# w_out loaded a second time, one byte further, in a fused convolution and SoLU kernel

## The chip, the cores and the metric

The kernel runs on 1 core of a Trainium2 chip. The time is the device time of one execution in microseconds (us). The kernel before takes 1151.21 us, the median of 3 runs (1150.63 to 1151.89).

Five engines work side by side, each through its own list of instructions in order: TensorE (PE; PEld is its weight load), VectorE (DVE), ScalarE (ACT), GpSimd (POOL) and SyncE (SP), which issues DMAs here.

## What is computed

```
w   = softmax(weight, over the 7 taps)                 # 8 heads x 7
x   = causal 7-tap convolution of x by w, head by head # 33280 tokens x 192
h   = x @ w_in                                         # 192 x 1024
sm  = exp(h - max h) / (sum + 1e-9)
s   = h * sm
ln  = (s - mean s) / sqrt(var s + 1e-6) * g_ln         # over 1024
out = (ln @ w_out) in float32                          # 1024 x 192
```

x, weight and g_ln are float32. w_in and w_out are float64; the kernel sees them as pairs of 32-bit words (low, high) and converts them itself.

## The kernel before, in words

The tokens are cut into 260 tiles of 128 (NT). For each tile TensorE multiplies the convolved rows by w_in in halves of float16 (`emit_rows` L747, `emit_first` L758, `emit_third` L779; the result `ph` is 128x1024 in PSUM); VectorE scales it and takes the maximum (`emit_max` L812, row L815), ACT the exponential (`emit_exp` L819, L822), VectorE the numerator (`emit_mul` L830, L832), ACT or POOL its upper half and POOL its lower half in float16 (`emit_hi` L837, `emit_lo` L857), SyncE turns both by a DMA transpose (`pT`, L860), TensorE multiplies by `ohl`, the halves of w_out (`emit_out` L877, L890), and VectorE empties the result. The accumulators in PSUM are three pairs of banks, so the product of tile 3 takes the pair of tile 0 and waits for that tile's numerator.

Every instruction's place in its engine's list is written out by hand (the schedule is manual): the program's order is each engine's order. `first_two`, `second_two`, `third_two` and `fourth_two` emit tiles 0 to 7 two by two, mixed with what is left of the start; then `three_steps` runs over three tiles at a time, and `last_three` ends it.

The start loads x for chunk 0, w_in (`raw_in`), and w_out (`raw_out`, L402), all from SyncE; then, later, x for chunks 1 and 2 with g (`gl`, L653) between them. A double becomes a float32 in class `Words`. For w_out, `wo`, in this order: `exponents` (VectorE, L467: the exponent bits of the high word), `powers` (ACT, L507: the power of two they stand for), `lows` (POOL, L478: the low word as a float), `mantissas` (VectorE, L472: 20 bits of the high word and the leading one), `floats` (ACT, L484: that integer as a float), `whole` (POOL, L495: plus the low word), `signs` (VectorE, L510: the sign bit into the power), `out_powers` (ACT, L702: eight products of the power by g, one for each block of 128 rows), `squares` (ACT, L490: the sum of squares, from which the scale `t_out` follows), `value` (POOL, L517: float times power, in two halves). From `out_scale` on, TensorE takes the mean over the rows of w_out (L718), VectorE subtracts it (L727), ACT and VectorE make the two halves `ohl` (L732, L736).

The order that the change touches is in `first_two`: `emit_first`, the maximum and exponential of tile 0, then `mantissas`, `floats`, `whole` and `signs` of w_out, the numerator of tile 0, `out_powers`, the maximum and exponential of tile 1, `squares`, the upper half of tile 0, `settle_rest` (VectorE's lower halves of the second part of chunk 0, L329, and their transposes into `yT`), the numerator of tile 1.

Buffers turn by tag. Tag `xs` has two: `raw_in`, then `f_in`; then `f_out` takes that of `raw_in`. Tag `g_raw` has three, for the exponents and mantissas of w_in and w_out and later for results.

Of the kernel before, what the change touches and what calls it, by code (L numbers as in the profile page):

```python
# [9 lines left out]
F32 = mybir.dt.float32  # L10
BF16 = mybir.dt.bfloat16
I32 = mybir.dt.int32
U32 = mybir.dt.uint32
AF = mybir.ActivationFunctionType
# [6 lines left out]
def kernel(  # L21
# [10 lines left out]
    P = 128  # L32
# [345 lines left out]

    w_in, w_out = w_in.bitcast(I32), w_out.bitcast(I32)
# [28 lines left out]
    rebias = cp.tile([P, 1], F32, name="rebias")  # L408
    pool.memset(rebias, -916.0 * 2.0**23)
    act.activation(rebias[0:1], rebias[0:1], AF.Copy)  # L410
    mhalf = cp.tile([P, 1], F32, name="mhalf")
# [35 lines left out]
    class Words:  # L447


        def __init__(self, raw, name):  # L450
# [4 lines left out]
            self.f = xp.tile(  # L455
                [P, NWM * D], F32, name=f"f_{name}", tag="xs", bufs=2
            )[:, 0:n]

        def exponents(self, c):
            if self.e is None:  # L460
                self.e, self.m = (
                    sp.tile(
                        [P, GMAX * D], I32, name=f"{q}_{self.name}", tag="g_raw", bufs=3
                    )[:, 0 : self.n]
                    for q in "em"
                )
            dve.tensor_scalar(  # L467
                self.e[:, c], self.high[:, c], 0x7FF00000, None, ALU.bitwise_and
            )
# [7 lines left out]
        def lows(self, c, scale):  # L477
            pool.tensor_scalar(  # L478
                self.low[:, c].bitcast(F32), self.low[:, c], scale, 1.0,
                ALU.mult, ALU.mult,  # L480
            )

        def floats(self, c):
            act.copy(self.m[:, c].bitcast(F32), self.m[:, c])  # L484

        def squares(self, c, to):
# [3 lines left out]
            act.activation(  # L490
                junk, self.e[:, c].bitcast(F32), AF.Square, scale=2.0**20, accum_out=to
            )

        def whole(self, c):
            pool.tensor_tensor(  # L495
                self.f[:, c], self.m[:, c].bitcast(F32),
                self.low[:, c].bitcast(F32), ALU.add,
            )
# [7 lines left out]
        def powers(self, c):  # L506
            act.activation(self.e[:, c], self.e[:, c], AF.Relu, bias=rebias, scale=8.0)  # L507
# [11 lines left out]
    wi, A, Z = Words(raw_in, "in"), slice(0, F), slice(F, 3 * F // 2)  # L519
# [8 lines left out]
    def valued(c, eng=pool):  # L528

        wi.signs(c, wi.m)  # L530
        wi.value(c, wi.m, eng)
# [108 lines left out]
    wo, W = Words(raw_out, "out"), slice(0, NFC * D)  # L640
# [8 lines left out]
    valued(Z)  # L649
    settle(*spans0[0], got1)  # L650
# [32 lines left out]
    wo.lows(W, 2.0**-32)  # L683
# [8 lines left out]
    osq = cp.tile([P, 1], F32, name="osq")  # L692
# [4 lines left out]
    def out_powers():  # L697


        woe = wo.e.bitcast(F32).rearrange("p (c d) -> p c d", d=D)  # L700
        for j in range(NFC):
            act.activation(  # L702
                woe[:, j], woe[:, j], AF.Copy, scale=gl[:, j : j + 1]
            )
# [476 lines left out]
    def first_two():  # L1181
# [5 lines left out]
        wo.mantissas(W)  # L1187
        wo.floats(W)
        wo.whole(W)
        wo.signs(W, wo.e)  # L1190
        emit_mul(t)
        out_powers()
        emit_max(u)
        emit_exp(u)
        wo.squares(W, osq)
        emit_hi(t)
        settle_rest()
        emit_mul(u)
# [470 lines left out]
```

## Time and profile before

| | us |
|---|---|
| median of 3 runs | 1151.21 |
| the profiled execution, its own time | 1150.31 |
| its span (first to last instruction) | 1148.6 |
| TensorE busy | 1127.5 |
| VectorE busy | 994.3 |
| ScalarE busy | 989.2 |
| GpSimd busy | 891.9 |

The profile is one execution recorded by the hardware profiler. A busy time is the sum of an engine's instructions without its waits. A timeline lists instructions by start, adjacent ones of a kind merged with their count; in brackets is how long the engine stood idle before and what ended that. The granted clock is 1.00 of full speed in every stretch shown.

### The profile page before, as it was taken

Reading aid. Unit: us, or ns where it says so; the run is one execution under the profiler, and the core shown is the slowest. Engines: PE = TensorE matmul, PEld = TensorE weight load, DVE = VectorE, ACT = ScalarE, POOL = GpSimd, SP = SyncE. Lnnn points to the kernel's source line nnn. Section 1 sums busy time; section 2 is a strip of 40 time slices with the busy share of each in tenths; the row PEclk is TensorE's granted clock in tenths of the full one; section 3 lists DMA queues with packets and bytes.
Section 4 is the critical chain, followed back from the end, with each engine's and each line's share of the span. In section 5 each row is a group of like instructions: output and inputs, shape, how many; then the busy total and the mean of one; then the engine's idle time right before and its main releaser. Section 6 shows DMA issues by size and latency. Waiting matters only on the chain.

```text
span 1148.6 us, 22366 instructions
## 1 busy us (share of the span) xinstructions
PE 1127.5 (98%) x7729; PEld 688.3 (60%) x7729; DVE 994.3 (87%) x2024; ACT 989.2 (86%) x1789; POOL 891.9 (78%) x711
## 2 busy tenths in 40 slices
PE   5999999999999999999999999999999999999998
PEld 3675556665666566656666666565656666566556
DVE  8889898988888898888888988888888887888787
ACT  7888998888888888988889898888888889888885
POOL 3866899978788687888868788687888868855664
PEclk9999999999999999999999999999999999999999
DMA  7999999999999999999999999999999998989977
GB/s 228 189 187 184 200 210 205 215 209 210 199 210 205 192 211 200 218 188 210 199 197 197 211 201 204 195 211 202 193 211 194 205 196 164 182 161 189 190 154 179
DMA packets 727424, 226.95 MB, mean 198 GB/s; under 512 B 651647, under 2 KB 725903, under 8 KB 727311
## 3 DMA queue, kind: packets, MB, share of 16 engines
q1 hardware_dynamic: 727310, 225.53, 102.7%
q8 instruction: 60, 0.98, 0.3%
q14 instruction: 54, 0.43, 0.1%
HBM read 33.00 MB, written 25.56 MB: 51 GB/s over the span
## 4 chain that ended last, share of the span: by engine, by line
PE 89%; ACT 2%; DVE 2%; DMA 2%; POOL 2%; issue 1%; SPq 0%; DVEq 0%; ACTq 0%; POOLq 0%
PE po L890 41%; PE ph L753 37%; PE pc L288 6%; PE ph L782 5%; DMA pT<-p 1%; POOL p L858 1%; ACT sq L847 1%; DMA raw_in<-in_moe_w_in_dram 1%; POOL xs L250 1%; DVE ph L815 0%; ACT e L822 0%; DVE e L832 0%; POOL xr L247 0%; ACT p L843 0%; ACT e_out L702 0%
## 5 line engine op out<-in xcount | busy, mean ns | idle before, releaser
L858 POOL TENSOR_TENSOR p<-e,p 128x1024 f16<-128x1024 f32 x257 | 547.7, 2135 | 188.3 <-ACT p L843 187.4
L890 PE MATMUL po<-ohl,pT 128*128 128x192 f16 (+1 forms) x4264 | 539.5, 283 | 3.1 <-DVE raw L900 1.4
L890 PEld LDWEIGHTS <-pT 128*128 128x128 f16 x4264 | 384.2, 98 | 163.2 <-issue 4.1
L753 PE MATMUL ph<-whi,yT 128*128 128x512 f16 x1548 | 419.0, 380 | 1.5 <-DVE e L832 1.5
L815 DVE TENSOR_SCALAR_CACHE_REDUCE ph<-ph,cv 128x1024 f32<-128x1024 f32 x248 | 319.3, 1289 | 87.0 <-PE ph L782 68.8
L822 ACT ACTIVATE e<-ph,sm 128x1024 f32<-128x1024 f32 x260 | 289.1, 1112 | 99.8 <-DVE ph L815 92.2
L832 DVE SCALAR_TENSOR_TENSOR e<-ph,cv,e 128x1024 f32<-128x1024 f32 x248 | 317.1, 1279 | 24.4 <-ACT e L822 23.9
L753 PEld LDWEIGHTS <-yT 128*128 128x128 f16 x2064 | 192.9, 98 | 228.5 <-issue 35.3
L843 ACT CAST p<-e 128x1024 f16<-128x1024 f32 x245 | 254.3, 1038 | 25.9 <-DVE e L832 23.0
L847 ACT ACTIVATE sq<-e 128x1024 f32<-128x1024 f32 x260 | 273.2, 1051 | 0.2
L753 PE MATMUL ph<-wlo,yT 128*128 128x512 f16 x516 | 153.5, 379 | 0.0
L900 DVE TENSOR_REDUCE raw<-po 128x192 f32<-128x384 f32 x247 | 136.9, 554 | 15.6 <-PE po L890 15.3
L250 POOL TENSOR_TENSOR xs<-xr,xs 128x960 f16<-128x960 f32 (+1 forms) x56 | 107.5, 1919 | 1.3
L782 PE MATMUL ph<-wlo,yT 64*128 64x512 f16 x269 | 74.1, 380 | 0.0
L329 DVE SCALAR_TENSOR_TENSOR y<-pc,y 112x432 f16<-112x432 f32 (+5 forms) x140 | 72.2, 533 | 0.9 <-ACT y L320 0.7
L288 PE MATMUL pc<-xs,taps_hi 128*112 128x240 f16 (+1 forms) x448 | 72.9, 261 | 0.0
L320 ACT ACTIVATE y<-pc 112x432 f16<-112x432 f32 (+5 forms) x140 | 62.6, 468 | 10.0 <-PE pc L288 5.5
L782 PE MATMUL ph<-wlo,y 64*128 64x512 f16 x251 | 68.7, 380 | 0.0
L183 DVE TENSOR_REDUCE xa<-xr 128x1 f32<-128x384 f32 x112 | 66.7, 618 | 0.0
L288 PEld LDWEIGHTS <-taps_hi 128*112 128x112 f16 x448 | 52.3, 130 | 16.0
L247 POOL TENSOR_SCALAR xr<-xr,s 128x960 f32<-128x960 f32 (+1 forms) x56 | 57.4, 1025 | 3.3 <-ACT xs L241 0.4
L288 PE MATMUL pc<-xs,taps_lo 128*112 128x240 f16 (+1 forms) x224 | 58.5, 261 | 0.0
(155 smaller groups left out, 774.4 us busy)
## 6 DMA issues: line engine op xcount, KB each, us to landing
out_dram<-raw SPq DMA_DIRECT2D x127, 192.0 KB, 3.0
xr<-in_x_dram SPq DMA_DIRECT2D x41, 480.0 KB, 4.9
xr<-in_x_dram SPq DMA_DIRECT2D x22, 384.0 KB, 4.3
pT<-p SPq DMA_TRANSPOSE x263, 4.6
y<-yT SPq DMA_DIRECT2D x15, 140.0 KB, 2.8
y<-yT SPq DMA_DIRECT2D x15, 126.0 KB, 2.9
yT<-y SPq DMA_TRANSPOSE x102, 3.7
raw_out<-in_moe_w_out_dram SPq DMA_DIRECT2D x1, 1536.0 KB, 10.3
```

Of the source, the lines that this page charges most:

```text
L250: (2.1 * size + 0.2, lambda: pool.tensor_tensor(xl, r, h, ALU.subtract)),
L288: nc.tensor.matmul(o, tp[:, h + j, :], r, start=q == 0, stop=q == len(ops) - 1)
L753: nc.tensor.matmul(bank, lhs, w[:, r, n * 512 : (n + 1) * 512], start=start and j == 0, stop=stop and j == len(ops) - 1,)
L782: nc.tensor.matmul(banks_of(t)[n], y[q, t.off : t.off + P], wlo[q, 1, n * 512 : (n + 1) * 512], start=start, stop=not start,)
L815: dve.tensor_scalar(t.ph, t.ph, t.cv[:, 0:1], None, ALU.mult, ALU.min, accum_out=t.bias)
L822: act.activation(t.e, t.ph, AF.Exp, bias=t.bias, scale=-1.0, accum_out=grp.z[:, g : g + 1])
L832: dve.scalar_tensor_tensor(t.e, t.ph, t.cv[:, 3:4], t.e, ALU.mult, ALU.mult, accum_out=t.grp.s1[:, t.g : t.g + 1],)
L843: act.copy(t.p16[:, :, 0, :], t.halves)
L847: act.activation(junk, t.e, AF.Square, accum_out=t.grp.s2[:, t.g : t.g + 1])
L858: eng.tensor_tensor(t.p16[:, :, 1, :], t.halves, t.p16[:, :, 0, :], ALU.subtract)
L890: nc.tensor.matmul(t.po[:, 0:n], t.pT[:, a, :], w, start=j == 0, stop=j == len(ops) - 1)
L900: dve.tensor_reduce(t.grp.raw[:, t.g, :], t.po[:, 0 : 2 * D].rearrange("p (a d) -> p d a", a=2), AX.X, ALU.add,)
```

## The change

w_out is loaded a second time, now from ACT's queue, into a tile `raw_top` of which the DMA fills the bytes from 1 on. The second word of each pair of words there (`shifted`) holds bytes 3 to 6 of the double, that is the lower 24 bits of its high word and the upper 8 of its low word: 28 bits of the mantissa in one word. `tops` on VectorE masks them and sets the leading one; `floats` turns this integer to a float on ACT, in eight pieces with g as the scale. So `lows`, `whole`, `mantissas` (for w_out) and `out_powers` go, and the float is written over the integers. `rebias_out` moves the exponent by 8 for the larger integers. The sum of squares is now taken of the powers without g, scaled by the largest g times 2^28 (`out_largest`: one reduction of `gl` on VectorE, one scaling on POOL). In `first_two` the numerator of tile 0 and the maximum of tile 1 come ahead of `signs`, and the numerator of tile 1 ahead of `settle_rest`. The load is issued behind the two `whi` rows of w_in on ACT; its buffer is that of `raw_in` (tag `xs`).

```diff
+    out_bytes = w_out.bitcast(U8)
...
+    fixed = cp.tile([P, 3], F32, name="fixed")
+    rebias, rebias_out, mhalf = (fixed[:, j : j + 1] for j in range(3))
...
+    pool.memset(rebias_out, -924.0 * 2.0**23)
...
-        def lows(self, c, scale):
...
-        def floats(self, c):
-            act.copy(self.m[:, c].bitcast(F32), self.m[:, c])
...
+        def tops(self, c):
+            dve.tensor_scalar(
+                self.m[:, c], self.shifted[:, c], 0xFFFFFFF, 0x10000000,
+                ALU.bitwise_and, ALU.bitwise_or,
+            )
+
+        def floats(self, c, by):
+            act.activation(self.f[:, c], self.m[:, c], AF.Copy, scale=by)
...
-        def whole(self, c):
...
-    wo, W = Words(raw_out, "out"), slice(0, NFC * D)
+    raw_top = xp.tile([P, NWM * D], I32, name="raw_top", tag="xs", bufs=2)
+    shifted = raw_top[:, 0 : 2 * NFC * D].rearrange("p (f t) -> p f t", t=2)[..., 1]
+    wo, W = Words(raw_out, "out", rebias_out, shifted), slice(0, NFC * D)
...
     for c in halves:
         act.activation(whi[:, 0, c], wi.f[:, c], AF.Copy, scale=t_in)
     valued(Z)
+    act.dma_start(
+        raw_top.bitcast(U8)[:, 1 : 1 + 8 * NFC * D].rearrange("p (c b) -> p c b", c=NFC),
+        out_bytes.rearrange("(c p) b -> p c b", p=P),
+    )
...
-    wo.lows(W, 2.0**-32)
...
-    def out_powers():
...
+    def out_floats():
+
         for j in range(NFC):
-            act.activation(
-                woe[:, j], woe[:, j], AF.Copy, scale=gl[:, j : j + 1]
-            )
+            wo.floats(slice(j * D, (j + 1) * D), gl[:, j : j + 1])
+
+    def out_squares():
+
+        wo.squares(W, osq, gm)
+
+    def out_largest():
+
+        dve.tensor_reduce(gm, gl, AX.X, ALU.max, apply_absolute_value=True)
+        pool.tensor_scalar(gm, gm, 2.0**28, 1.0, ALU.mult, ALU.mult)
...
         emit_exp(t)
-        wo.mantissas(W)
-        wo.floats(W)
-        wo.whole(W)
+        wo.tops(W)
+        out_largest()
+        out_floats()
+        emit_mul(t)
+        emit_max(u)
         wo.signs(W, wo.e)
-        emit_mul(t)
-        out_powers()
-        emit_max(u)
         emit_exp(u)
-        wo.squares(W, osq)
+        out_squares()
+        emit_mul(u)
         emit_hi(t)
         settle_rest()
-        emit_mul(u)
         emit_hi(u)
```

## Rows read from the trace of the kernel before

**Rows 1.** The page: the first line, and the line of busy time, share of the span and instructions of each engine.

```profile
span 1148.6 us, 22366 instructions
PE 1127.5 (98%) x7729; PEld 688.3 (60%) x7729; DVE 994.3 (87%) x2024; ACT 989.2 (86%) x1789; POOL 891.9 (78%) x711
```

**Rows 2.** The view of waits for TensorE over the whole span: engine and line that waited, engine and line waited for; us in total, times, longest us.

```profile
PE ph L753 <- DVE e L832: 1.5, 1, 1.5
PE pc L288 <- issue: 1.7, 1, 1.7
PE po L890 <- DVE raw L900: 1.4, 2, 0.9
PE po L890 <- DMA pT<-p: 1.1, 3, 0.4
```

**Rows 3.** The timeline of TensorE between 27 and 45 us: start us, duration us, engine, line, operation, out<-in, shape, count, and in brackets the idle time before with what ended it. The second row is the first output product (tile 0), the third that of tile 1.

```profile
27.93 0.61 PE L753 MATMUL ph<-whi,yT 128*128 128x512 f16 x2 [1.48 <-DVE e L832]
...
41.66 2.15 PE L890 MATMUL po<-ohl,pT 128*128 128x192 f16 x24 [0.24 <-ACT xj L189]
...
44.36 2.15 PE L890 MATMUL po<-ohl,pT 128*128 128x192 f16 x24 [0.40 <-DMA pT<-p]
```

**Rows 4.** The chain of waits in the first 60 us: start us, us, what.

```profile
26.70 2.88 ACT e_out L702 x8
...
39.52 0.45 DVE ohl L736
```

**Rows 5.** The timeline of VectorE from 22 to 42 us, columns as in rows 3. L815 is the maximum of a tile (tiles 1 and 2), L832 its numerator (tiles 0 and 1), L329 the lower halves of chunk 0, L727 and L736 the centring of w_out and its low half.

```profile
23.83 1.18 DVE L472 TENSOR_SCALAR m_out<-raw_out 128x1536 int32<-128x1536 int32 x1
24.93 1.74 DVE L510 SCALAR_TENSOR_TENSOR e_out<-raw_out,e_out 128x1536 int32<-128x1536 int32 x1
26.59 1.27 DVE L832 SCALAR_TENSOR_TENSOR e<-ph,cv,e 128x1024 f32<-128x1024 f32 x1
...
27.79 1.28 DVE L815 TENSOR_SCALAR_CACHE_REDUCE ph<-ph,cv 128x1024 f32<-128x1024 f32 x1
...
29.00 1.46 DVE L329 SCALAR_TENSOR_TENSOR y<-pr,s,y 112x480 f16<-112x480 f32 x3
30.70 1.28 DVE L832 SCALAR_TENSOR_TENSOR e<-ph,cv,e 128x1024 f32<-128x1024 f32 x1 [0.25 <-ACT e L822]
...
31.91 1.29 DVE L815 TENSOR_SCALAR_CACHE_REDUCE ph<-ph,cv 128x1024 f32<-128x1024 f32 x1
...
37.57 1.81 DVE L727 SCALAR_TENSOR_TENSOR f_out<-f_out,mean 128x768 f32<-128x768 f32 x2
39.52 1.95 DVE L736 SCALAR_TENSOR_TENSOR ohl<-f_out,t_out,ohl 128x768 f16<-128x768 f32 x2
```

**Rows 6.** The timeline of GpSimd (POOL) from 20 to 45 us and, last, TensorE's mean of w_out; columns as in rows 3.

```profile
22.57 1.62 POOL L478 TENSOR_SCALAR raw_out<-raw_out 128x1536 f32<-128x1536 uint32 x1
26.70 3.54 POOL L495 TENSOR_TENSOR f_out<-m_out,raw_out 128x1536 f32<-128x1536 f32 x1 [2.52 <-issue]
...
30.41 3.58 POOL L517 TENSOR_TENSOR f_out<-f_out,e_out 128x768 f32<-128x768 f32 x2
...
33.95 2.85 PE L718 MATMUL mean<-f_out,even 128*128 128x192 f32 x16
```

**Rows 7.** The timeline of ScalarE (ACT) from 14 to 36 us, and POOL's row that it waits for; columns as in rows 3.

```profile
15.83 1.33 ACT L648 ACTIVATE whi<-f_in,t_in 128x512 f16<-128x512 f32 x2 [0.45 <-DVE t_in L114]
16.73 1.26 POOL L517 TENSOR_TENSOR f_in<-f_in,m_in 128x512 f32<-128x512 f32 x1 [0.63 <-DVE m_in L510]
18.03 2.94 ACT L660 ACTIVATE whi<-f_in,t_in 64x512 f16<-64x512 f32 x4 [0.87 <-POOL f_in L517]
...
25.11 1.46 ACT L484 CAST m_out<-m_out 128x1536 f32<-128x1536 int32 x1
```

**Rows 8.** DMA. First from the page: the queues that carried data, and the issue of raw_out (KB, us from issue to landing). Then SyncE's timeline (start us, us of the issue). Then busy times by stretches: the stretch, its length, the busy time of each engine, the granted TensorE clock, the share of the 16 DMA engines' time in which they were busy, GB/s. Last the packets of the stretch from 24.75 to 25.75 us.

```profile
q1 hardware_dynamic: 727310, 225.53, 102.7%
...
raw_out<-in_moe_w_out_dram SPq DMA_DIRECT2D x1, 1536.0 KB, 10.3
...
5.72 0.42 SPq L402 DMA_DIRECT2D raw_out<-in_moe_w_out_dram  x1
...
20.16 1.14 SPq L162 DMA_DIRECT2D xr<-in_x_dram  x2
21.35 0.52 SPq L653 DMA_DIRECT2D gl<-in_moe_g_ln_dram  x1
...
12.00:15.00 3.00, 2.38 (x15) 2.08 (x15) 2.67 (x10) 2.65 (x8) 0.54 (x1) 1.00 1.05 366
15.25:15.50 0.25, 0.25 (x5) 0.25 (x4) 0.20 (x2) 0.13 (x1) 0.25 (x1) 1.00 0.09 31
17.20:18.50 1.30, 0.84 (x4) 0.33 (x5) 1.30 (x4) 0.47 (x1) 0.79 (x1) 1.00 0.00 0
18.50:22.50 4.00, 2.97 (x11) 0.62 (x9) 3.50 (x7) 3.91 (x8) 0.41 (x3) 1.00 0.53 98
21.25:21.50 0.25, 0.06 (x1) 0.07 (x2) 0.25 (x1) 0.25 (x1) 0.00 (x0) 1.00 0.27 40
22.50:25.75 3.25, 3.25 (x15) 1.12 (x14) 3.13 (x4) 3.07 (x4) 1.69 (x2) 1.00 1.15 303
...
DMA packets 1303, 0.19 MB, mean 194 GB/s; under 512 B 1056, under 2 KB 1303, under 8 KB 1303
```

More of the change, by code (lines that the diff above doesn't have):

```diff
@@ L13 @@
 U32 = mybir.dt.uint32
+U8 = mybir.dt.uint8
 AF = mybir.ActivationFunctionType
@@ L405 @@
     )
-    rebias = cp.tile([P, 1], F32, name="rebias")
+    fixed = cp.tile([P, 3], F32, name="fixed")
+    rebias, rebias_out, mhalf = (fixed[:, j : j + 1] for j in range(3))
     pool.memset(rebias, -916.0 * 2.0**23)
     act.activation(rebias[0:1], rebias[0:1], AF.Copy)
-    mhalf = cp.tile([P, 1], F32, name="mhalf")
+    pool.memset(rebias_out, -924.0 * 2.0**23)
     pool.memset(mhalf, -0.5)
@@ L447, with __init__ @@
     class Words:
-        def __init__(self, raw, name):
+        def __init__(self, raw, name, bias, shifted=None):
+            self.bias, self.shifted = bias, shifted
             self.name = name
@@ L454, in __init__ @@
             self.n, self.e = n, None
-            self.f = xp.tile(
-                [P, NWM * D], F32, name=f"f_{name}", tag="xs", bufs=2
-            )[:, 0:n]
+            if shifted is None:
+                self.f = xp.tile(
+                    [P, NWM * D], F32, name=f"f_{name}", tag="xs", bufs=2
+                )[:, 0:n]
         def exponents(self, c):
@@ L466, in exponents @@
                 )
+                if self.shifted is not None:
+                    self.f = self.m.bitcast(F32)
             dve.tensor_scalar(
@@ L475, in mantissas, with squares @@
             )
-        def lows(self, c, scale):
-            pool.tensor_scalar(
-                self.low[:, c].bitcast(F32), self.low[:, c], scale, 1.0,
-                ALU.mult, ALU.mult,
-            )
-        def floats(self, c):
-            act.copy(self.m[:, c].bitcast(F32), self.m[:, c])
-        def squares(self, c, to):
+        def tops(self, c):
+            dve.tensor_scalar(
+                self.m[:, c], self.shifted[:, c], 0xFFFFFFF, 0x10000000,
+                ALU.bitwise_and, ALU.bitwise_or,
+            )
+        def floats(self, c, by):
+            act.activation(self.f[:, c], self.m[:, c], AF.Copy, scale=by)
+        def squares(self, c, to, scale=2.0**20):
             junk = sp.tile([P, F], F32, name=f"oj_{self.name}_{c.start}", tag="sq", bufs=1)
@@ L490, in squares @@
             act.activation(
-                junk, self.e[:, c].bitcast(F32), AF.Square, scale=2.0**20, accum_out=to
-            )
-        def whole(self, c):
-            pool.tensor_tensor(
-                self.f[:, c], self.m[:, c].bitcast(F32),
-                self.low[:, c].bitcast(F32), ALU.add,
+                junk, self.e[:, c].bitcast(F32), AF.Square, scale=scale, accum_out=to
             )
@@ L506, in powers @@
         def powers(self, c):
-            act.activation(self.e[:, c], self.e[:, c], AF.Relu, bias=rebias, scale=8.0)
+            act.activation(self.e[:, c], self.e[:, c], AF.Relu, bias=self.bias, scale=8.0)
         def signs(self, c, to):
@@ L517, in value @@
             eng.tensor_tensor(f, f, powers[:, c].bitcast(F32), ALU.mult)
-    wi, A, Z = Words(raw_in, "in"), slice(0, F), slice(F, 3 * F // 2)
+    wi, A, Z = Words(raw_in, "in", rebias), slice(0, F), slice(F, 3 * F // 2)
     HF = F // 2
@@ L682 @@
     wo.powers(W)
-    wo.lows(W, 2.0**-32)
+    both = cp.tile([P, 2], F32, name="gm_osq")
+    gm, osq = both[:, 0:1], both[:, 1:2]
     def settle_rest():
@@ L691 @@
     t_out = cp.tile([P, 1], F32, name="t_out")
-    osq = cp.tile([P, 1], F32, name="osq")
     wof = wo.f.rearrange("p (c d) -> p c d", d=D)
@@ L695 @@
     out_halves = [slice(0, NFC * D // 2), slice(NFC * D // 2, NFC * D)]
-    def out_powers():
-        woe = wo.e.bitcast(F32).rearrange("p (c d) -> p c d", d=D)
+    def out_floats():
         for j in range(NFC):
-            act.activation(
-                woe[:, j], woe[:, j], AF.Copy, scale=gl[:, j : j + 1]
-            )
+            wo.floats(slice(j * D, (j + 1) * D), gl[:, j : j + 1])
[4 more added lines that the diff above has]
+        pool.tensor_scalar(gm, gm, 2.0**28, 1.0, ALU.mult, ALU.mult)
     def out_scale():
```

## The prediction

> **What bounds the kernel now.** I read the page's busy times first. TensorE is busy 1127.5 of 1148.6 us [rows 1]: the kernel can hardly gain in its body, and what it can gain or lose lies in TensorE's pauses. The view of what TensorE waited for puts nearly all of them before 45 us; of its waits on the output products only 1.4 and about 0.7 us come later (its three waits for `pT` total 1.1, of which one of 0.4 is at 44.36) [rows 2, 3]. Since the body is TensorE-bound, a microsecond by which the first output products move is a microsecond of the whole.
>
> So the change must be judged in the start, where tiles 0 to 3 share the engines with the conversion of `w_out`. TensorE's row list shows it there waiting for others: 1.48 us for tile 0's numerator (L832), 0.24 and 0.40 us ahead of the first two output products [rows 3]. Who is late? The chain of waits runs over ACT's multiplication by g at 26.70 and DVE's low half of `ohl` at 39.52 [rows 4]. VectorE's own rows settle it: from 23.83 to the end of that low half at 41.47 they stand end to end, with one listed pause of 0.25 us inside [rows 5]. VectorE's queue carries the start; ACT and POOL matter only when a VectorE row has to wait for them.
>
> **What goes.** On POOL the low words (1.62 us) and the sum of halves (3.54 us) vanish [rows 6], on ACT the cast of 1.46 us, since the eight multiplications by g (2.88 us for all, 0.36 each) now read the integers themselves [rows 4, 7]. I value all of this at nothing. POOL has no row that holds VectorE up here: its value of `f_out` (3.58 us from 30.41) feeds the mean at 33.95, but the mean is only used at 37.57, when VectorE has finished both numerators [rows 5, 6]. After the change the value waits for `signs`, and 3.58 us of POOL and 2.85 us of mean need some 6.5 us between the end of `signs` and L727. VectorE's own work there covers it: 6.87 us from tile 1's numerator at 30.70 to L727 at 37.57, and the 1.46 us of lower halves that now stand there too. Without that cover the mean would be the next to be late.
>
> **What stays on VectorE.** The top words cost what the mantissas cost (L472, a step of 1.10 us from 23.83 to 24.93): same form, same stride. The maximum of g, a 128x8 reduction, has no row; its nearest are the small reductions and scalars of the same view at 0.15 to 0.21 us, I take 0.2. `signs` (a step of 1.66 us, 24.93 to 26.59) only moves behind the maximum of tile 1. If everything had landed, tile 0's numerator could then start once tile 0's exponential is through (25.1, when ACT's next row starts), not at 26.59; but the list from there to the maximum of tile 2 then holds `signs` again. Before: numerator at 26.59, maximum of tile 2 at 31.91, so 5.32 us, of which 0.25 is a pause. After: 5.32 - 0.25 + 1.66 = 6.73 us [rows 5, 7]. From tile 2's maximum on VectorE's list is the same as before. With data in hand the start ends within 0.1 us of where it does now, and only the 0.40 us at the second output product is there to win: at best about -0.4 us. Work is taken from the engines that wait, none from the one that is waited for.
>
> **What is added: two landings in VectorE's way.** The extra memset and the 128x1 scaling of the maximum on POOL lie in idle time there. The second load is 1536 KB. Its buffer is the one of `raw_in`, free after VectorE's last `signs` of w_in, which ends at about 16.65 (the value of that piece starts on POOL at 16.73). ACT issues it behind the two `whi` rows, which end at 17.16; ACT then stands until 18.03 in any case [rows 7]. SyncE's issues of such loads take about 0.5 us [rows 8]; ACT's are not in this trace (one dynamic queue is used), so between 0 and 0.87 us it costs nothing, and I take it as free.
>
> When does it land? SyncE's load issued at 20.16 shows its first packets at about 21.35, 1.2 us later; the same delay here gives 18.4. The load of `raw_out` moved at 366 GB/s with all 16 DMA engines busy, so 1.573 MB are 4.30 us of them. From 17.2 to 18.5 they are free, from 18.5 to 22.5 busy for 0.53 of the time with `yT` transposes and the first x rows: 0.1 + 0.47 x 4.0 = 2.0 us. After 22.5 they are full (1.15). So 2.3 us of the load are left over when the x rows of chunk 1, and behind them g, want the same engines [rows 8].
>
> And g is now waited for on VectorE. Its load is issued on SyncE at 21.35 behind two x loads; its 1024 packets of 4 bytes are the 1056 small ones of 24.75 to 25.75. In the kernel before only ACT at 26.70 needs it, and it does not wait. After, the reduction of g stands between the top words and tile 0's numerator. Whichever of the two streams the engines prefer, both are through only after 25.75 + 2.3 = 28.05; with about 0.5 us to landing (`raw_out`'s packets end at 15.5, it landed at 5.72 + 10.3 = 16.0) that is 28.55 [rows 8]. If g is last, 0.2 us follow, if the top words are last, 1.3 us: the numerator starts at 28.8 to 29.9, I take the middle, 29.3.
>
> By the Trainium skill, "DMA: Bandwidth & Descriptors", section "Issuing engines are not separate DMA queues", a load issued by another engine runs on the same 16 DMA engines and interleaves with the rest, so that only issue time is saved; no run here shows two queues. By it the sum stands as it is; without it the load would cost what the first rival below does.
>
> Behind the waiting top words are queued on VectorE tile 0's numerator, tile 1's maximum, `signs`, tile 1's numerator and the lower halves of chunk 0; TensorE (tile 3 needs tile 0's numerator), ACT and POOL wait for those. **The sum**: (29.3 - 26.59) + (1.66 - 0.25) = 4.1 us at the maximum of tile 2, and as much at the first output product, 41.66; less the 0.40 us at the second product, whose transpose is then no longer last: +3.7 us. The bounds of the same sum are 28.8 and 29.9: +3.2 and +4.3. The transposes of `yT` that tile 0 needs may come up to 1 us later by the sharing, which the wait of the top words covers. The profiled run took 1150.31 us (its span and 1.7 us around it), 0.9 us under the median; on the median of 1151.21 the forecast is 1154.9.
>
> **Rivals.** *The load fits into the gaps*: not slower. If it never holds up g, g still lands at 25.75 + 0.4, the reduction ends at 26.35, and the sum is 26.35 - 26.59 + 1.41 - 0.4 = +0.8 us, 1152.0. The place is the reduction of g on VectorE; it decides as long as the numerator of tile 0 starts before 27.9, where the sum reaches 2.3 us, 0.2%, about what a measurement of this kernel tells from no change. For it: the engines are free about half of the time until 22.5, and in what order they serve two streams is in no row. Against it: nothing before 17.16 can start it, and whichever stream goes first, the other is the later by it.
>
> *The odd address halves the rate.* All loads of this trace start on whole words, so none prices it. At twice 4.30 us (an assumed factor, the mildest that would matter much), 6.6 us would be left at 22.5, the top words would start at 25.75 + 6.6 + 0.5 = 32.85, the numerator at 34.2, and the sum is 7.6 + 1.41 - 0.4 = +8.6 us: 1159.8. The Trainium skill, "DMA: Bandwidth & Descriptors", section "How a descriptor splits into AXI transactions", says that a descriptor starting off a 256-byte boundary needs a further transaction; it says so of reads, and no row here shows it for a write. Seven for six would by estimate add 0.7 us, 1155.6.
>
> *The delay is paid back.* TensorE waits for 2.1 us on others after 45 us; if those releasers are not delayed as much, since POOL and ACT have 6.6 us less to do, at most these come back: +1.6 us, 1152.8. Against it: the delayed engine is the one that feeds all of them.
>
> *Faster.* TensorE's pauses between 27 and 45 us are 2.1 us and the 1.7 us ahead of the convolution L288 [rows 2, 3], and VectorE's list sets when they end; 2.3 us would need VectorE itself to run quicker. The mantissas took 1.18 us beside POOL, and the passes that leave POOL cover 5.2 us; even a fifth less of that is 1.0 us, which with the first rival gives -0.2 us.
>
> **How the numbers follow.** The forecast 0.50; the load in the gaps 0.26; half rate 0.13; paid back 0.07; faster by more than 0.2% by something that I don't see 0.04. Slower is 0.50 + 0.13 = 0.63, same 0.26 + 0.07 = 0.33, faster 0.04. The range goes from just under the first rival's 1152.0 to the half-rate case: 1151.6 to 1160.0.
>
> **What would show it.** Right: in the profile after, VectorE has a pause of 3 to 5 us ahead of the top words or of the reduction of g, ended by a DMA; tile 0's numerator starts near 29.3; the first output product near 45.8; ACT's load is issued near 17.2 without delaying the row at 18.03; POOL stands idle longer, without effect. Wrong: the top words start before 26, or the load takes over 12 us to land, or TensorE's pauses after 45 us shrink by what the start lost.

## The result, and the profile after

The changed kernel took 1157.2 us (median of 6 runs, 1156.56 to 1159.03), the kernel before 1151.55 us in the 6 runs beside them (1150.63 to 1153.8): ratio 1.0051, 95% interval 1.0041 to 1.0061, so 5.65 us slower. Forecast was 1154.9 us within 1151.6 to 1160.0, with slower as the likeliest. Sign and range held; the size was 2 us short, and the profile shows that the wait on which the sum stood is not the one that was paid. That the number came so near is in good part luck.

The profiled run of the changed kernel took 1159.03 us around a span of 1157.3. The two spans differ by 8.7 us, since this run lies 1.8 us over the median of its kernel and the profiled run of before (1150.31 us) 1.2 us under its own. Times inside the trace are therefore read as to where the loss sits, the timed runs as to how much it is.

First TensorE, since the body hangs on it: its waits over the whole span (engine and line that waited, engine and line waited for; us in total, times, longest us), and its timeline (start us, us, engine, line, operation, out<-in, shape, count, idle before).

```profile
PE ph L777 <- DMA yT<-y: 5.5, 2, 4.1
PE po L902 <- DMA pT<-p: 3.2, 1, 3.2
...
PE po L902 <- DVE raw L912: 1.4, 2, 0.9
PE ph L765 <- DVE e L844: 1.0, 1, 1.0
```

```profile
24.14 1.89 PE L777 MATMUL ph<-whi,yT 128*128 128x512 f16 x4 [4.14 <-DMA yT<-y]
...
48.84 4.02 PE L902 MATMUL po<-ohl,pT 128*128 128x192 f16 x24 [3.18 <-DMA pT<-p]
...
52.99 2.97 PE L902 MATMUL po<-ohl,pT 128*128 128x192 f16 x24
```

Two waits are new or many times longer: 4.1 us for a transpose of y (`yT`, the input of tile 0's logits), and 3.2 us for the transpose of tile 0's weights (`pT`). Both are transfers that the change does not touch. The first output product starts at 48.84 where it started at 41.66, the second at 52.99 where it started at 44.36 [rows 3]: +7.2 and +8.6 us, and with the second the difference of the spans is complete. The waits for `raw` are the same 1.4 us as before [rows 2]: what follows 55 us was not changed.

Next VectorE, whose list the prediction followed. L827 is a tile's maximum, L485 the top words, L715 the new reduction of g, L844 a tile's numerator, L511 the signs, L330 the lower halves of chunk 0.

```profile
14.67 0.15 DVE L647 TENSOR_REDUCE isq<-pt_wi 128x1 f32<-128x3 f32 x1
...
27.02 1.29 DVE L827 TENSOR_SCALAR_CACHE_REDUCE ph<-ph,cv 128x1024 f32<-128x1024 f32 x1 [5.15 <-PE ph L794]
...
28.23 0.96 DVE L485 TENSOR_SCALAR m_out<-raw_top 128x1536 int32<-128x1536 int32 x1
29.10 0.15 DVE L715 TENSOR_REDUCE gm_osq<-gl 128x1 f32<-128x8 f32 x1
29.72 1.28 DVE L844 SCALAR_TENSOR_TENSOR e<-ph,cv,e 128x1024 f32<-128x1024 f32 x1 [0.46 <-ACT e L834]
...
32.13 1.75 DVE L511 SCALAR_TENSOR_TENSOR e_out<-raw_out,e_out 128x1536 int32<-128x1536 int32 x1
33.81 1.27 DVE L844 SCALAR_TENSOR_TENSOR e<-ph,cv,e 128x1024 f32<-128x1024 f32 x1
...
35.01 1.46 DVE L330 SCALAR_TENSOR_TENSOR y<-pr,s,y 112x480 f16<-112x480 f32 x3
36.39 1.28 DVE L827 TENSOR_SCALAR_CACHE_REDUCE ph<-ph,cv 128x1024 f32<-128x1024 f32 x1
```

The pause of 5.15 us stands one step earlier than forecast: ahead of tile 0's maximum, not ahead of the top words, and it ends with TensorE's logits. Top words and reduction of g follow without any wait: both loads had landed. The same rows of the kernel before, to set beside them (the first is the reduction of a norm of w_in that stands ahead of all that the change touches, the second the maximum of tile 0):

```profile
14.89 0.15 DVE L644 TENSOR_REDUCE isq<-pt_wi 128x1 f32<-128x3 f32 x1
...
22.62 1.29 DVE L815 TENSOR_SCALAR_CACHE_REDUCE ph<-ph,cv 128x1024 f32<-128x1024 f32 x1 [0.52 <-PE ph L782]
```

The starts of the executions differ: that reduction stands at 14.67 to 16.53 us in the profiles of this study. Where stages of several kernels are compared below, I count from it. Tile 0's maximum is at 22.62 - 14.89 = 7.73 us before, and at 27.02 - 14.67 = 12.35 after: 4.6 us later. In the trace's own times, tile 0's numerator stands at 29.72 (forecast 29.3), tile 2's maximum at 36.39 instead of 31.91 [rows 5]: +4.5 (forecast +4.1). The numbers fit, by another cause: the pause is not VectorE's wait for a landing.

That cause is on the DMA side. First the load's issue on ACT with ACT's next `whi` row (timeline of ACT), then the issues (KB, us from issue to landing), then packets, MB and share of the 16 engines of each queue between 19 and 22 us: after (first two lines), and the same stretch before (last fence). q10 is the queue of the new load, q1 that of SyncE, where all other data goes.

```profile
16.46 0.42 ACTq L653 DMA_DIRECT2D raw_top<-in_moe_w_out_dram  x1
17.81 2.94 ACT L667 ACTIVATE whi<-f_in,t_in 64x512 f16<-64x512 f32 x4 [0.87 <-DVE y L330]
```

```profile
raw_top<-in_moe_w_out_dram ACTq DMA_DIRECT2D x1, 1536.0 KB, 7.2
...
gl<-in_moe_g_ln_dram SPq DMA_DIRECT2D x1, 4.0 KB, 6.0
```

```profile
q10 hardware_dynamic: 723, 1.11, 102.7%
q1 hardware_dynamic: 28, 0.01, 1.1%
```

```profile
q1 hardware_dynamic: 1108, 0.30, 55.5%
```

The issue cost ACT nothing (`whi` follows at 17.81, before at 18.03 [rows 7]). The load landed at 16.46 + 7.2 = 23.7 us, 4.6 us before VectorE came to it. But while it ran, SyncE's queue had 28 packets in 3 us, all of them after 21.5 us, where it had 1108 before. The chain of waits (start us, us, what) shows what stood there:

```profile
17.38 6.71 DMA yT<-y
41.24 7.55 DMA pT<-p
```

The transpose of y issued at 17.38 took 6.71 us; before, the one issued at 18.90 landed in 2.49, and the one ahead of it in 2.5. In the kernel before, TensorE went on with tile 0's logits at

```profile
21.44 0.61 PE L765 MATMUL ph<-whi,yT 128*128 128x512 f16 x2 [0.69 <-DMA yT<-y]
```

after it did so at 24.14, 2.7 us later, and from there to the maximum it took 2.9 us instead of 1.2, with four instead of two of the large matmuls left and, as the next view shows, at half the clock: 4.4 us in all in the trace's own times, 4.6 counted from the reduction. The busy times of three stretches (stretch, length, busy time of each engine, granted clock, DMA share, GB/s) show both the full engines and what TensorE ran at behind its waits:

```profile
18.50:22.50 4.00, 1.18 (x4) 0.29 (x3) 3.28 (x6) 3.91 (x8) 0.53 (x3) 1.00 1.02 345
24.00:27.00 3.00, 2.86 (x7) 0.60 (x8) 0.00 (x0) 0.00 (x0) 0.00 (x0) 0.50 1.14 319
48.00:52.90 4.90, 4.06 (x26) 3.86 (x27) 1.50 (x4) 3.58 (x8) 4.73 (x5) 0.50 1.08 235
```

After 4.1 us of standing, and again after 3.2, TensorE was granted 0.50 of its clock, the 1.2 GHz level: the first two output products took 4.02 and 2.97 us instead of 2.15 each (the second ran at the lower level only in part).

The second new wait begins on SyncE. Its timeline after, and then that of the kernel before:

```profile
27.65 11.20 SPq L360 DMA_TRANSPOSE yT<-y  x3
38.90 0.59 SPq L695 DMA_DIRECT2D wlo<-wlo  x1
39.59 0.51 SPq L154 DMA_DIRECT2D xr<-in_x_dram  x1
40.16 0.99 SPq L163 DMA_DIRECT2D xr<-in_x_dram  x2
41.24 14.88 SPq L872 DMA_TRANSPOSE pT<-p  x5
```

```profile
26.35 6.19 SPq L359 DMA_TRANSPOSE yT<-y  x3
32.59 0.59 SPq L687 DMA_DIRECT2D wlo<-wlo  x1
...
36.11 12.84 SPq L860 DMA_TRANSPOSE pT<-p  x4
```

The lower halves of chunk 0 now stand behind tile 1's numerator, at 35.01 instead of 29.00 [rows 5]. SyncE's transposes of them, a copy of `wlo` and three x loads wait for them in SyncE's order, and tile 0's `pT` stands behind these: issued at 41.24 instead of 36.11, and landed 7.55 us later, among the x loads. Not all of this is the queue's. POOL makes the lower halves of `pT`'s input, two tiles in a row (the kernel before first, then after):

```profile
33.96 4.21 POOL L858 TENSOR_TENSOR p<-e,p 128x1024 f16<-128x1024 f32 x2
37.59 4.21 POOL L870 TENSOR_TENSOR p<-e,p 128x1024 f16<-128x1024 f32 x2
```

Tile 0's is the first of the two, 2.12 us long: POOL was through with it at 36.08 before and at 39.71 after. So of the 7.2 us by which the first output product is late, 3.6 come from the delay that POOL inherits, 1.5 are SyncE's queue (41.24 - 39.71; before, the issue followed within 0.1 us), and 2.0 the longer landing (7.55 instead of 5.5).

### The profile page after: what moved, and what is told of

Same layout as the page of the kernel before. It is cut to its first block, busy times and chain, and to the rows that moved or that the text cites. A ratio compares the mean times of both kernels' runs of the same rounds, so it can differ in the third digit from the quotient of the medians.

```text
span 1157.3 us, 22369 instructions
## 1 busy us (share of the span) xinstructions
PE 1131.1 (98%) x7729; PEld 691.3 (60%) x7729; DVE 993.8 (86%) x2025; ACT 988.1 (85%) x1788; POOL 887.1 (77%) x711
## 3 DMA queue, kind: packets, MB, share of 16 engines
q10 hardware_dynamic: 1040, 1.57, 0.4%
## 4 chain that ended last, share of the span: by engine, by line
PE 91%; DVE 3%; ACT 2%; DMA 2%; issue 1%; SPq 0%; DVEq 0%; POOL 0%; ACTq 0%
PE po L902 42%; PE ph L765 37%; PE pc L289 6%; PE ph L794 6%; DVE ph L827 1%; DVE e L844 1%; ACT sq L859 1%; DMA pT<-p 1%; DMA yT<-y 1%; ACT e L834 1%; DMA raw_in<-in_moe_w_in_dram 1%; DVE y L330 0%; DVE xa L184 0%; ACT xs L242 0%; ACT p L855 0%
## 5 line engine op out<-in xcount | busy, mean ns | idle before, releaser
L827 DVE TENSOR_SCALAR_CACHE_REDUCE ph<-ph,cv 128x1024 f32<-128x1024 f32 x248 | 319.4, 1289 | 93.5 <-PE ph L794 75.3
L844 DVE SCALAR_TENSOR_TENSOR e<-ph,cv,e 128x1024 f32<-128x1024 f32 x248 | 317.0, 1279 | 23.5 <-ACT e L834 23.2
L330 DVE SCALAR_TENSOR_TENSOR y<-pc,y 112x432 f16<-112x432 f32 (+5 forms) x140 | 72.2, 533 | 0.2 <-ACT y L321 0.2
```

Of the source, the lines that this page charges most:

```text
L827: dve.tensor_scalar(t.ph, t.ph, t.cv[:, 0:1], None, ALU.mult, ALU.min, accum_out=t.bias)
L844: dve.scalar_tensor_tensor(t.e, t.ph, t.cv[:, 3:4], t.e, ALU.mult, ALU.mult, accum_out=t.grp.s1[:, t.g : t.g + 1],)
```

## The experiments

Three theories were set against each other: A, the load's bytes hold up the transposes of y; B, the prediction's, VectorE waits for the landings of the load and of g; C, the moved lower halves keep SyncE's queue shut for tile 0's `pT`. Every kernel was timed beside the kernel before; ratios are to that, with their 95% interval.

| run | edit, in words | us | before, us | ratio |
|---|---|---|---|---|
| e1_no_load | after, without the load | 1153.46 | 1152.05 | 1.0013 [1.0005, 1.0022] |
| e2_load_odd | before, with the load alone | 1155.08 | 1152.05 | 1.0026 [1.0015, 1.0037] |
| e3_load_even | the same, at an even address | 1155.53 | 1152.05 | 1.0033 [1.0020, 1.0045] |
| e4_settle_first | after, lower halves not moved | 1156.19 | 1152.05 | 1.0035 [1.0021, 1.0049] |
| e5_load_behind | after, load behind the transposes | 1158.06 | 1151.38 | 1.0056 [1.0044, 1.0068] |
| e6_all_three | e5, g early, lower halves not moved | 1154.80 | 1151.38 | 1.0029 [1.0018, 1.0040] |
| e7_settle_late | before, with the lower halves moved | 1155.34 | 1151.38 | 1.0035 [1.0023, 1.0047] |
| e8_signs_late | before, with the signs moved | 1154.95 | 1151.38 | 1.0030 [1.0019, 1.0042] |
| e9_no_load_settle_first | e1, lower halves not moved | 1151.53 | 1152.00 | 0.9997 [0.9988, 1.0006] |
| e10_no_load_g_early | e9, and g early | 1151.17 | 1152.00 | 0.9990 [0.9981, 0.9999] |
| e11_half_load | e2 with half of the load | 1152.19 | 1152.00 | 1.0004 [0.9995, 1.0012] |

**The load taken away** (e9 and e10 share this edit):

```
-    raw_top = xp.tile([P, NWM * D], I32, name="raw_top", tag="xs", bufs=2)
-    shifted = raw_top[:, 0 : 2 * NFC * D].rearrange("p (f t) -> p f t", t=2)[..., 1]
+    shifted = raw_out[..., 1]
...
-    act.dma_start(
-        raw_top.bitcast(U8)[:, 1 : 1 + 8 * NFC * D].rearrange("p (c b) -> p c b", c=NFC),
-        out_bytes.rearrange("(c p) b -> p c b", p=P),
-    )
```

> The changed kernel without its second load: the top words are taken from the high words of the first load, so the values are not the reference's; every other part of the change stays. Theory A (the load's bytes hold up the transposes of yT, and this is the whole loss): back to the kernel before, within 1.2 us of it, the maximum of tile 0 near 22.5 us. Theory B (what the load costs is VectorE's wait for its landing): also near the kernel before, but then with g's landing in VectorE's way, +0.8 us, the numerator of tile 0 near 26.3. Theory C (the moved lower halves push SyncE's queue: the transposes, the copy of wlo and the x loads of chunk 3 now stand ahead of pT of tile 0): +2 to +4 us, pT of tile 0 issued near 38 us instead of 36.1 and TensorE waiting over 1 us for it.

It took 1.4 us more than before instead of 5.65; A and B had expected up to 1.2 and C 2 to 4. Tile 0's maximum is back at 7.78 us from the reduction of the norm (before 7.73), without a wait for `yT`. Of the rest, VectorE's timeline and TensorE's show two waits, B's in its small form and C's:

```profile
27.63 0.16 DVE L710 TENSOR_REDUCE gm_osq<-gl 128x1 f32<-128x8 f32 x1 [1.16 <-DMA gl<-in_moe_g_ln_dram]
```

```profile
46.03 3.81 PE L897 MATMUL po<-ohl,pT 128*128 128x192 f16 x24 [2.38 <-DMA pT<-p]
```

The wait for g is that of the prediction's first rival (a load without price, +0.8 us).

**The load alone.** Into a buffer that nobody reads, in the kernel before, at the change's odd address (below), and at an even one, with 0 in the place of both 1:

```
+    spare = xp.tile([P, NWM * D], I32, name="spare", tag="xs", bufs=2)
     valued(Z)
+    act.dma_start(
+        spare.bitcast(U8)[:, 1 : 1 + 8 * NFC * D].rearrange("p (c b) -> p c b", c=NFC),
+        out_bytes.rearrange("(c p) b -> p c b", p=P),
+    )
     settle(*spans0[0], got1)
```

> The kernel before, with the second load of w_out added at the same place in ACT's queue and at the same odd address, into a buffer that nobody reads; f_out takes the other buffer of its tag. Theory A: +4 to +6 us, the transposes of yT land 4 us later and the maximum of tile 0 starts near 27 us. Theory B: within 1 us of the kernel before, since nothing waits for the load. Theory C: within 1 us too, since no instruction of the start is moved.

> As e2_load_odd, but the bytes go to offset 0 instead of 1. If the odd address costs nothing: the load lands 7 us after its issue as in the changed kernel, and the time is that of e2_load_odd within 0.7 us. If the odd address costs a further transaction in six, the load lands about 0.7 us earlier and the time is 0.7 us less; if it halves the rate, 3 to 4 us less.

Nothing waits for this load, and it costs 3.0 us (A had expected 4 to 6, B and C under 1). From e2 the load's issue row and the rows of TensorE and VectorE behind it:

```profile
spare<-in_moe_w_out_dram ACTq DMA_DIRECT2D x1, 1536.0 KB, 7.4
```

```profile
25.22 1.89 PE L772 MATMUL ph<-whi,yT 128*128 128x512 f16 x4 [4.32 <-DMA yT<-y]
```

```profile
28.11 1.29 DVE L822 TENSOR_SCALAR_CACHE_REDUCE ph<-ph,cv 128x1024 f32<-128x1024 f32 x1 [5.33 <-PE ph L789]
```

The wait for `yT` is there, and tile 0's maximum is at 12.53 us from the reduction (after: 12.35). So A is shown: the bytes alone, on the other queue, make the first wait. At the even address the load landed after 7.2 us instead of 7.4, and the time is within the noise of e2's (+3.5): the odd address costs nothing that can be measured (in the changed kernel, at the odd address too, the load landed after 7.2).

**The lower halves put back.** In the changed kernel, settle_rest again ahead of tile 1's numerator:

```
         out_squares()
-        emit_mul(u)
         emit_hi(t)
         settle_rest()
+        emit_mul(u)
         emit_hi(u)
```

> The changed kernel with the lower halves of the second part of chunk 0 and their transposes back ahead of the numerator of tile 1. Theory A: the time of the changed kernel within 1 us. Theory C: 2 to 3 us less than the changed kernel, pT of tile 0 issued within 0.2 us of the end of POOL's subtraction, and TensorE's wait for it under 1 us.

The wait for `pT` is gone, the first output product starts 33.0 us after the reduction of the norm (after: 34.2), and both products take their 2.15 us:

```profile
49.44 2.15 PE L902 MATMUL po<-ohl,pT 128*128 128x192 f16 x24
...
51.60 2.14 PE L902 MATMUL po<-ohl,pT 128*128 128x192 f16 x24
```

The time is +4.1 instead of +5.65 us; the intervals of the two overlap (1.0021 to 1.0049 and 1.0041 to 1.0061), so by these alone the gain is likely, not certain; C had expected 2 to 3 us. The edit also has a price, in a place that the prediction had named: without the lower halves as cover the mean is the next to be late, and VectorE waits 0.71 us for it.

```profile
44.99 1.82 DVE L739 SCALAR_TENSOR_TENSOR m_out<-m_out,mean 128x768 f32<-128x768 f32 x2 [0.71 <-PE mean L730]
```

The same edit without the load says the same:

> As e1_no_load (top words from the first load, values not the reference's), with the lower halves of chunk 0 back ahead of the numerator of tile 1. If the load (A), the wait for g (B) and SyncE's queue behind the moved lower halves (C) are the whole cost, what is left is the sign bits between the numerator of tile 0 and the maximum of tile 2: TensorE's 2.4 us wait for pT of e1_no_load falls under 1 us and the time is 0 to +0.8 us from the kernel before, about 1 us under e1_no_load. If more than +1.5 us is left, the order itself costs something that is not named yet.

e9 ends at 0.9997 where e1 had 1.0013 (upper end of the one 1.0006, lower end of the other 1.0005): 1.9 us for the order of one group of instructions, by medians. Two pairs of kernels point the same way, and in both the wait for `pT` goes with the edit. C is a part of the loss.

**The load behind the transposes.** SyncE issues it, behind the three transposes of y:

```
-    act.dma_start(
+    settle(*spans0[0], got1)
+    nc.sync.dma_start(
         raw_top.bitcast(U8)[:, 1 : 1 + 8 * NFC * D].rearrange("p (c b) -> p c b", c=NFC),
         out_bytes.rearrange("(c p) b -> p c b", p=P),
     )
-    settle(*spans0[0], got1)
```

> The changed kernel with one edit: the second load is issued by SyncE behind the three transposes of yT and ahead of the x loads of chunk 1, in their own queue. Theory A (the transposes starve behind the load's packets): they land as in the kernel before, TensorE's 4 us wait for yT is gone and the maximum of tile 0 starts 7.7 us after the reduction of isq, as in the kernel before (12.4 in the changed one). Theory B's wait must then appear: VectorE waits some 2 us for the load and then 2 to 4 us more for g, whose own load now stands behind 1.5 MB more; the time is 4 to 5.5 us over the kernel before. If A is wrong, the wait for yT stays.

The wait for `yT` is gone (tile 0's maximum at 7.73 us again), and now B's waits appear, both of them, on VectorE:

```profile
28.45 0.96 DVE L485 TENSOR_SCALAR m_out<-raw_top 128x1536 int32<-128x1536 int32 x1 [3.47 <-DMA raw_top<-in_moe_w_out_dram]
31.34 0.16 DVE L715 TENSOR_REDUCE gm_osq<-gl 128x1 f32<-128x8 f32 x1 [1.93 <-DMA gl<-in_moe_g_ln_dram]
```

The cost is the same or more, +6.7 us (expected was less). The bytes have to pass between 16 and 29 us, and here too the stream that is served second is waited for: this is the picture that the prediction drew, in the kernel in which SyncE's queue orders it so.

**All three at once.** e5 with g loaded by ACT at the very start instead of by SyncE behind chunk 1's x, and with the lower halves put back as in e4:

```
     gl = cp.tile([P, NFC], F32, name="gl")
+    act.dma_start(gl, g_ln.rearrange("(c p) -> p c", p=P))
...
         chunks[1].load(j)
-    nc.sync.dma_start(gl, g_ln.rearrange("(c p) -> p c", p=P))
```

> As e5_load_behind, and with g loaded by ACT at the very start, and the lower halves of chunk 0 back ahead of the numerator of tile 1. If A (starved transposes), B (landings in VectorE's way) and C (SyncE's queue behind the moved lower halves) are the whole cost, only the wait for the load itself is left: it lands about 2.5 us after VectorE is ready, the maximum of tile 2 starts some 2.5 us later than in the kernel before, and the time is 1.5 to 2.5 us over it, 3 to 4 us under the changed kernel. If something else costs, it stays over +3 us.

Less was expected than the +3.4 us measured. VectorE waits once, 3.39 us for the load at the top words. TensorE still waits 1.48 us for `pT`, though the lower halves are back in their place: SyncE, which now carries the load too, issued it at 40.66, 1.0 us after POOL had finished its input (39.68). So the moved lower halves are not the only thing that can make this queue late. Neither of the two places tried for the 1.5 MB is free of cost.

**The moved instructions alone, in the kernel before.**

```
+        emit_mul(u)
         emit_hi(t)
         settle_rest()
-        emit_mul(u)
         emit_hi(u)
```

> The kernel before with one part of the change alone: the numerator of tile 1 goes ahead of the lower halves of chunk 0 and their transposes. Theory C: +0.5 to +1.5 us, SyncE issues the transposes of pT of tile 0 1 to 2 us after POOL has finished its halves, and TensorE waits over 1 us for pT. Theory A and B: within 0.5 us.

It cost +4.0 us, much more than expected, and it is no clean copy of C: the lower halves had also filled the time until tile 1's exponential, and VectorE now waited 1.57 us for that at 32.23. The wait for `pT` is there, 1.97 us, and the output products behind it took 2.76 and 3.05 us. The spread of its runs was the widest of all (1152.94 to 1158.68), and the profiled run lies 2.1 us over their median: TensorE was granted 0.58 of its clock in it from 20 to 24 us, ahead of anything that the edit moves. The 4.0 us are therefore no price of C.

```
         wo.whole(W)
-        wo.signs(W, wo.e)
         emit_mul(t)
-        out_powers()
         emit_max(u)
+        wo.signs(W, wo.e)
         emit_exp(u)
+        out_powers()
```

> The kernel before with only the order products, then signs: the numerator of tile 0 and the maximum of tile 1 go ahead of the sign bits on VectorE, the exponential of tile 1 ahead of the products by g on ACT; no second load. By the prediction's step that VectorE's list carries the start, the maximum of tile 2 starts within 0.3 us of where it does in the kernel before and the time is within 0.5 us of it. If instead the numerator of tile 0 sets the pace, as TensorE's 1.48 us wait for it suggests, 1 to 1.5 us are won.

This was expected at nothing or a little, and cost +3.6 us. VectorE's row of the signs and the row of POOL beside it:

```profile
29.04 4.16 DVE L510 SCALAR_TENSOR_TENSOR e_out<-raw_out,e_out 128x1536 int32<-128x1536 int32 x1
```

```profile
28.04 3.54 POOL L495 TENSOR_TENSOR f_out<-m_out,raw_out 128x1536 f32<-128x1536 f32 x1 [2.51 <-issue]
```

The signs took 4.16 us instead of 1.74 [rows 5]: issued 1.0 us into POOL's sum of halves, they ended 1.62 us after its end (28.04 + 3.54 = 31.58; 29.04 + 4.16 = 33.20), as if they had stood until it was through. In the changed kernel that sum is gone, POOL is idle from 29.84 to 34.04, and the signs took 1.75 us. In e8 tile 2's maximum came 2.4 us later than before (19.47 us from the reduction of the norm, before 17.02). The rest of the cost has a second source: in e8 ACT's products by g still read the signed powers, so that they started only at 33.23, after 2.81 us of waiting for the signs, and behind them VectorE waited 1.42 us for the sum of squares. In the changed kernel the products read the integers and start ahead of the signs. So "products, then signs" is cheap there because the sum of halves left POOL and the products no longer need the signs: the relief of POOL that the prediction valued at nothing pays for a part of the new order. How large a part, no run separates.

**What the change is worth without the price of its bytes.**

> As e9_no_load_settle_first, with g loaded by ACT at the very start. This is the change without any price of its loads. By the prediction's step that VectorE's list carries the start, so that POOL's 5.2 us and ACT's 1.5 us less are worth nothing, the maximum of tile 2 starts within 0.4 us of where it does in the kernel before, counted from the reduction of isq (17.0 us), and the time is -0.6 to +0.3 us from it. If the freed engines matter, it is over 1.2 us faster.

e9 with g loaded as in e6: 1151.17 against 1152.0, ratio 0.9990 with an upper end of 0.9999: about 0.8 us, and hardly outside the noise. VectorE waits neither for the load nor for g, and tile 2's maximum stands 17.08 us from the reduction of the norm where it stood at 17.02 before.

**Half of the load.** The edit of e2, but

```
-        spare.bitcast(U8)[:, 1 : 1 + 8 * NFC * D].rearrange("p (c b) -> p c b", c=NFC),
-        out_bytes.rearrange("(c p) b -> p c b", p=P),
+        spare.bitcast(U8)[:, 1 : 1 + 4 * NFC * D].rearrange("p (c b) -> p c b", c=NFC // 2),
+        out_bytes[0 : F // 2].rearrange("(c p) b -> p c b", p=P),
```

> As e2_load_odd, with half of the bytes (768 KB in one DMA, rows 0 to 511). If the transposes of yT stand until the load's packets are through, they are late by what is left of 2.2 us of packets: the load lands near 5 us after its issue and the maximum of tile 0 starts 0.5 to 1.5 us later than in the kernel before, counted from the reduction of isq (7.7 us); the time is +0 to +1 us. If the two queues take turns and each transpose is slowed in proportion to the bytes, the delay is half of e2's 4.8 us, 2 to 3 us, and the time +1.5 us.

TensorE's wait for `yT` was 1.52 us and tile 0's maximum came 1.84 us later, at 9.57; between 20 and 21 us the load's queue had 217 packets and SyncE's none, between 21.5 and 22 SyncE's had 295. The delay lies between the two that were expected (0.5 to 1.5 if the transposes stand until the load's packets are through, 2 to 3 if the queues take turns); the time, 1.0004 [0.9995, 1.0012], is that of the first. In the profile its second output product starts 47.44 - 15.53 = 31.9 us after the reduction of the norm, 2.4 later than before, which the timed runs don't show. The profiled run of before is a quick one, 1150.31 us where the medians of that kernel beside these runs are 1151.38 to 1152.05; and in e10, timed 0.8 us under before, that product stands 30.05 us from the reduction, 0.6 later than in that profile. So some 1 us of the 2.4 may belong to the profile of before. Whether some of the rest is paid back is left open.

## Why the prediction was right, and where it was not

**TensorE bounds the body, a microsecond of the start is a microsecond of the whole.** Right. The second output product starts at 44.36 before, 46.20 in e10, 49.16 in e2, 51.60 in e4 and 52.99 after; the spans are 1148.6, 1149.9, 1152.8, 1155.2 and 1157.3 us. Their differences to that start lie within 0.8 us (1103.6 to 1104.3). In the other profiles it is 1103.4 to 1104.7 us, but for e7 (1106.2), which lost more behind that point.

**The work that goes is worth nothing, at best -0.4 us.** Right as a sum, within the noise (e10: about -0.8, by its interval -2.2 to -0.1, with no landing waited for), but the reason was too short: e8 shows that POOL's sum of halves would have held up the moved signs for 2.4 us.

**ACT's issue is free, the odd address is a rival.** Right: `whi` was not delayed; e2 and e3 show no price for the address, so the half-rate rival is out.

**The waits.** This step failed: "The transposes of `yT` that tile 0 needs may come up to 1 us later by the sharing, which the wait of the top words covers." It took the two queues to share the engines, so that transposes and x rows keep their 0.53 of the time until 22.5 and the load takes the rest. The engines served the load nearly alone (723 packets to 28), it was early by 4.6 us, and the transposes were late: tile 0's maximum came 4.4 us later (2.7 of landing, 1.7 of matmuls piled up behind it at half the clock), one step ahead of where VectorE was to wait. So the term of 2.7 us for VectorE's landings was not paid at all, and one that the prediction had put at nothing, the transposes', took its place with 4.4. That the sum came out near is luck as far as the mechanism goes. A reason for it may be that the same bytes have to pass whichever stream is behind (e5, the other order, cost +6.7); the prediction said so of g and the load, and ought to have put the transposes of y among the streams. That the bytes alone set the loss is not shown: half of them (e11) cost nothing that can be measured. The rule that it cited from the Trainium skill ("DMA: Bandwidth & Descriptors", "Issuing engines are not separate DMA queues") holds here as far as the 16 engines are the same; that the streams interleave is seen in this trace only as the load runs out, after 21.5 us.

**The terms that were missing.** The forecast counted the moved lower halves as 1.46 us on VectorE, with the same end of the list at tile 2's maximum. It did not count what SyncE issues behind them (three transposes, the copy of `wlo`, three x loads) ahead of tile 0's `pT`: the first output product came at 48.84 in the profiled run, 7.2 us late, where 45.8 was forecast, 4.1 late. e9 against e1 prices the move at 1.9 us, e4 against after at 1.0 to 1.5. Nor did it count the lower clock behind TensorE's waits. In after, and in e1 and e7, the output products behind this wait also ran at the lower clock in part; in e4, without the wait, they did not, nor in e5, with a wait of 2.35 us.

**The account.** Four kernels make a square, each against the kernel before: no load and the lower halves in their place -0.5 us (e9), no load and the lower halves moved +1.4 (e1), the load and the lower halves in their place +4.1 (e4), both +5.65 (after, interval 4.7 to 7.0). So in the changed kernel the load costs 4.2 to 4.6 us and the move 1.5 to 1.9, and the rest of the change nothing that can be measured. In the kernel before, the same load cost 3.0 to 3.5 us (e2, e3), about 1 us less. The late landing of g is no separate term in after (no wait there); it shows only in e1 (1.16 us), e9 (0.51) and e5 (1.93), where the load does not delay tile 0's maximum. Each of these differences is uncertain by more than 1 us, and whether the load really costs more in the changed kernel, the runs don't tell.

Of the rivals, "the load fits into the gaps" is out: e1 is the kernel in which the load has no price, with that rival's wait for g, and the changed kernel is 4.2 us over it; "paid back" is not seen in the waits for `raw` (1.4 us before and after).

## What to carry to other kernels

When a transfer is added on another queue, list every small transfer that the same DMA engines must deliver in that stretch, transposes above all, and ask of each who is late if the new bytes all go first, and who if they go last; the order chooses who shows the loss, and in the two orders tried here it was about the same (5.65 and 6.7 us). When an engine's step is moved, write out what other queues issue behind it in program order, down to the first transfer that TensorE waits for. And an engine relieved off the critical path may be worth next to nothing by itself (here at most some 0.8 us), and still be part of what makes another move possible.

## What the runs showed of the hardware

- Two DMA queues did not share evenly: while 1.5 MB ran on ACT's queue, SyncE's moved 28 packets in 3 us (1108 before), all of them after 21.5 us, and the transpose waiting there took 6.71 us; behind 0.75 MB (e11) SyncE's queue came back as the load's packets ran out. The Trainium skill, "DMA: Bandwidth & Descriptors", section "Queues, rings and completion order", says that each DMA engine goes round between the queues it has work for, packet by packet, and that such a packet is a group of descriptors, typically 9 to 17 and at most 64. The profile's packets of the load are single rows of `w_out` (1.11 MB in 723 is 1536 bytes each), 1024 in all, by estimate 64 for each of the 16 engines. If one packet in the Trainium skill's sense held many such rows, taking turns would look much like this; how the rows were grouped no run here tells, so the counts neither show that rule nor refute it. Whether SyncE's transposes had handed over little work at a time, or the engines preferred the load, is open too.
- A load of 1.5 MB into SBUF at an odd byte address landed after 7.4 us (e2), at an even one after 7.2 (e3).
- A VectorE pass with two operands in SBUF stood behind POOL's sum for some 2.4 us (e8). The Trainium skill, "SBUF — State Buffer", section "Who interferes with whom", says that such a pass contends with a POOL instruction that reads SBUF, that the ports which the two share are an exclusive lock, and that the order of issue decides who blocks; the rows of e8 agree (POOL's sum at 28.04, the signs at 29.04, 4.16 us long instead of 1.74).
- TensorE was granted 0.50 of its clock after standing for 3 to 4 us. It cost where TensorE was the late one: the output products ran in it (4.02 and 2.97 us instead of 2.15), and so did tile 0's last logits (four large matmuls 1.89 us, 1.03 at the full clock). In e2 the granted clock was 0.51 from 24 to 29 us and 0.56 from 29 to 35, in e3 0.66 and 1.00, and e2 was not the slower (1155.08 and 1155.53 us). The clock also fell without so long a stand: in e7 it was 0.58 from 20 to 24 us, where TensorE had stood no longer than in the kernel before (1.37 and 0.29 us; before 1.36 and 0.29).
